# Part of a folded weight product placed inside attention's tiles

## The chip, the cores and the metric

The kernel runs on one core of a Trainium2 chip. The metric is device time in microseconds for one execution; three runs are given, and a profile of one further execution.

## The reference

Three layers follow one another, all in float32:

```python
# attention: 4 batches, 8 heads, 768 positions, 64 wide
state = gamma * state + outer(k[t], v[t]);  y[t] = scale * q[t] @ state
# mixture of experts: 3072 tokens of 512, 8 experts, 1024 wide inside
e = argmax(x @ w_gate + modality_bias[modality_id])
x = gate * (relu(x @ w1[e]) @ w2[e])
# last layer
out = ((x @ m_w1) * (x @ m_w2)) @ w3 @ w_out
```

Nothing stands between `w3` and `w_out`, so the kernel multiplies these two weights with each other ahead of time. This is the folded weight product.

## The kernel before

Attention works on 24 tiles of 128 positions, six to a batch. In a loop over tiles (lines 514 to 556) iteration t issues, in this order: the loads for tile t+6; `vprime` (values times a decay, GpSimd) for t+2; `scores(t+1)` on TensorE, masked by VectorE into `at`; `rows_gate(t-1)`, which turns the output `xT` into rows and gate logits; `attend_T` (queries times state) and `attend_v` (masked scores times values) of tile t, which go into one bank, from which VectorE scales them by a decay table into `xT` (line 333); and `state(t+1)`, whose sum ScalarE copies into `T`. Each engine takes its instructions in the order in which they were issued. A tile that begins a batch has no `attend_T`, and one that ends it has no `state`.

`rows_gate` has ScalarE copy the rows out and send them to HBM from its own queue. Its VectorE sum gives the gate logits `L`. After tiles 8, 15 and 21 of the count a batch of logits is routed: `route_a` and, an iteration later, `route_b` run as blocks of small VectorE operations, with two small products between. GpSimd then scatters each tile's tokens to their list positions in HBM (`scatter_ids`, line 398, 8 bytes a token).

The weights `w_out` and `w3` come as float64 bits in twelve chunks of 1 MB (0 to 3 and 4 to 11). VectorE decodes a chunk in three operations (lines 196, 198, 200). ScalarE casts it to a high part, and GpSimd or VectorE forms the low part. Seven chunks are decoded in attention's loop, five behind it. The folded product has 64 units of three 128x128x512 matmuls (line 245), eight units to a bank. All 64 run behind attention, in the fold stage:

```python
fold_mm(FM[0]); route_b(t0, t1)   # 6 units, then the last three tiles' routing
...                               # scatters, tables1 (list gather), one chunk decoded
tables2a(); fold_mm(FM[1]); tables2b()
...                               # first expert's weights, two chunks
fold_mm(FM[2]); tables3(); gather_x(0); gather_x(1)
...
t_x(0); fold_mm(64)               # the units that are left
```

`tables1` gathers the token lists from HBM by `ridx` (line 434), `tables2b` transposes the control table `c`, and `tables3` transposes the lists into gather indices. Then the first expert slot begins (line 234). Expert slots, the last layer's products and a tail follow.

PSUM has eight banks: five that `bank()` hands out in turn, one for the state and two for `rows_gate`.

## Time and profile before

| | us |
|---|---|
| median of three runs | 890.35 (890.24 to 890.61) |
| the profiled execution, its own time | 890.2 |
| its span, first to last instruction | 888.1 |
| TensorE matmul busy | 845.1 (95%) |
| VectorE busy | 479.6 (54%) |
| GpSimd busy | 341.7 (38%) |
| ScalarE busy | 287.8 (32%) |

Stretches are given in microseconds from the start of the span. Matmuls overlap in the pipeline, so the time from one start to the next says what one costs, not its length. PE is TensorE, DVE is VectorE, ACT is ScalarE, POOL is GpSimd, SP is SyncE, and a releaser is what ended an engine's idle time.

### The profile page before, as it was taken

The page shows a single profiled execution, that of the slowest core. Times are in us where ns is not written, and L with a number is a line of the kernel's source. Part 1 is how long each engine was busy: PE and PEld are TensorE (multiplying, and loading weights), DVE is VectorE, ACT ScalarE, POOL GpSimd, SP SyncE. Part 2 cuts the span into 40 slices and gives each one's busy share as a digit, 9 for nine tenths or more (in the row PEclk, how much of TensorE's full clock was granted, in tenths as well). Part 3 has the DMA queues.
Part 4 walks back from the last instruction along what each step waited for, and adds up shares of the span by engine and source line. Part 5 has one row for each costly group of instructions (what it writes and reads, how often), then busy time and mean ns, then how long its engine had stood idle before and what let it go on. Part 6 is the DMA issues. An engine that isn't in the chain of part 4 may idle for free. (4 is left out here: it accounts for less than half of the span.)

```text
span 888.1 us, 16214 instructions
## 1 busy us (share of the span) xinstructions
PE 845.1 (95%) x6240; PEld 771.9 (87%) x6240; DVE 479.6 (54%) x697; ACT 287.8 (32%) x514; POOL 341.7 (38%) x324
## 2 busy tenths in 40 slices
PE   5989798899999999999999979999999999999997
PEld 5978687679999999899999957887887888999996
DVE  4477675764432516751111662255236375999993
ACT  1232231143213233623111633232223353455541
POOL 4237374123005041804000314246326354656563
PEclk9998999999999999999999999999999999999999
DMA  8999974778236445744235039514111514644411
GB/s 297 348 389 232 337 183 109 202 265 314 88 121 214 144 169 191 275 179 180 84 96 216 26 123 410 218 48 147 63 51 60 148 51 146 225 168 154 143 49 59
DMA packets 63189, 153.68 MB, mean 173 GB/s; under 512 B 10676, under 2 KB 22964, under 8 KB 61545
## 3 DMA queue, kind: packets, MB, share of 16 engines
q1 hardware_dynamic: 51736, 122.64, 40.9%
q0 software_dynamic: 7888, 23.36, 7.5%
q10 hardware_dynamic: 3456, 6.29, 2.0%
q8 instruction: 61, 1.00, 0.5%
q14 instruction: 48, 0.39, 0.2%
HBM read 102.73 MB, written 49.58 MB: 171 GB/s over the span
## 5 line engine op out<-in xcount | busy, mean ns | idle before, releaser
L234 PE MATMUL b<-h,wh 128*128 128x256 f32 x768 | 139.7, 284 | 1.3 <-issue 0.7
L895 PE MATMUL al<-xh,ws 128*128 128x512 f32 x384 | 125.7, 397 | 5.3 <-PEq L868 3.6
L234 PEld LDWEIGHTS b<-h,wh 128*128 128x128 f32 x768 | 119.6, 192 | 1.7 <-issue 0.9
L759 DVE SCALAR_TENSOR_TENSOR h<-b,h 128x512 fp32r<-128x512 f32 x48 | 32.6, 689 | 157.7 <-ACT h L758 155.5
L234 PE MATMUL b<-xh,wl 128*128 128x256 f32 x384 | 108.7, 283 | 0.3 <-DVE wl L205 0.3
L234 PE MATMUL b<-xh,wh 128*128 128x256 f32 x384 | 108.8, 283 | 0.1
L234 PE MATMUL b<-h,wl 128*128 128x256 f32 x384 | 108.7, 283 | 0.1
L234 PE MATMUL b<-xl,wh 128*128 128x256 f32 x384 | 108.6, 283 | 0.0
L895 PEld LDWEIGHTS al<-xh,ws 128*128 128x128 f32 x384 | 73.0, 190 | 23.3 <-ACTq L868 3.8
L895 PE MATMUL al<-xl,ws 128*128 128x512 f32 x192 | 76.2, 397 | 0.0
L1095 PE MATMUL oa<-wfh,ab 128*128 128x256 f32 x384 | 75.0, 284 | 0.7 <-DVE ot L1102 0.6
L234 PEld LDWEIGHTS b<-xh,wl 128*128 128x128 f32 x384 | 73.6, 192 | 0.5 <-DVE wl L205 0.5
L234 PEld LDWEIGHTS b<-xh,wh 128*128 128x128 f32 x384 | 73.6, 192 | 0.4 <-issue 0.3
L234 PEld LDWEIGHTS b<-h,wl 128*128 128x128 f32 x384 | 73.6, 192 | 0.3 <-issue 0.3
L234 PEld LDWEIGHTS b<-xl,wh 128*128 128x128 f32 x384 | 73.6, 192 | 0.0
L1095 PEld LDWEIGHTS oa<-wfh,ab 128*128 128x128 f32 x384 | 61.6, 189 | 2.7 <-DVE ot L1102 2.2
L895 PE MATMUL ga<-xh,ws 128*128 128x512 f32 x192 | 63.4, 391 | 0.0
L758 ACT ACTIVATE h<-b 128x512 fp32r<-128x512 f32 x48 | 28.4, 597 | 86.4 <-PE b L234 84.9
L205 POOL TENSOR_TENSOR wo<-dec,wo 128x512 fp32r<-128x512 f32 x12 | 16.5, 1392 | 99.1 <-ACT wo L204 99.1
L1095 PE MATMUL oa<-wfl,ab 128*128 128x256 f32 x192 | 54.0, 281 | 0.0
L635 POOL DMA_INDIRECT xg<-x_scratch,gidx x28 | 28.4, 1014 | 64.6 <-PE b L644 44.4
L790 ACT COPY yT<-b 128x512 f32<-128x512 f32 x24 | 14.1, 589 | 118.3 <-PE b L234 110.7
(219 smaller groups left out, 1894.9 us busy)
## 6 DMA issues: line engine op xcount, KB each, us to landing
qkv<-in_qkv SPq DMA_DIRECT2D x22, 768.0 KB
ws_scratch<-wo SPq DMA_DIRECT2D x28, 512.0 KB
ws<-ws_scratch SPq DMA_DIRECT2D x28, 512.0 KB
raw<-in_wall SPq DMA_DIRECT2D x24, 512.0 KB
ab<-ab_scratch SPq DMA_DIRECT2D x24, 512.0 KB
f64f<-in_w SPq DMA_DIRECT2D x8, 1024.0 KB
f64m<-in_m SPq DMA_DIRECT2D x16, 512.0 KB
y_scratch<-yT SPq DMA_DIRECT2D x14, 512.0 KB
```

The source lines that it names most:

```text
L205: lo_eng.tensor_tensor(lo, src, hi.bitcast(F32), op=ALU.subtract)
L234: nc.tensor.matmul(b, lhsT=x, rhs=y, start=first and n == 0, stop=last and n == 3 * len(ks) - 1)
L635: nc.gpsimd.indirect_dma_start(out=xgs[j][y], out_offset=None, in_=xd, in_offset=bass.IndirectOffsetOnAxis(ap=gidx[:, y, j:j + 1], axis=0))
L758: nc.scalar.activation(h, b, AF.Relu)
L759: V.scalar_tensor_tensor(l, b, 0.0, h.bitcast(F32), op0=ALU.max, op1=ALU.subtract)
L790: nc.scalar.copy(yT[:, 2 * dp:2 * dp + 2, :].rearrange("p a t -> p (a t)"), b)
L895: nc.tensor.matmul(b, lhsT=y, rhs=r[:, kk, :], start=first and n == 0, stop=n == 5, skip_group_check=True)
L1095: nc.tensor.matmul(b, lhsT=x[:, k], rhs=y[:, k], start=first and n == 0, stop=n == 11, skip_group_check=True)
```

## The change

- Twelve chunks are loaded in attention's loop and ten are decoded there.
- From tile 15 on, each iteration issues three, three and two units of the folded product behind `scores`, 24 in all. They have a bank of their own, and four banks are handed out in turn.
- Decoding, the bias operations and routing become generators. `spend` issues their steps at the end of an iteration until the estimated costs reach `BUDGET[t]`.
- `decayed` scales the queries on VectorE ahead of `scores`, so `xT` (but for tile 0) is a plain copy by ScalarE.
- Row stores are issued by SyncE, with five buffers for three. Six loads of queries, keys and values are held instead of seven.
- Constants are loaded in pieces at the start, and the biases are formed from tile 3 on.
- The fold stage has 40 units and two chunks left, and `tables2a` follows `tables1` at once.

```diff
-LOAD_T = [2, 5, 8, 10, 13, 15, 18, 20, 22]
-SPLIT_T = [5, 8, 10, 13, 15, 18, 20]
-QB, KB, FB = 7, 5, 5
+LOAD_T = [1, 2, 5, 6, 8, 11, 12, 14, 16, 19, 21, 23]
+SPLIT_T = [3, 5, 7, 9, 11, 13, 15, 17, 19, 21]
+FOLD_T = 15
+FOLD_N = [3, 3, 2] * 3
+BUDGET = [2.0] * 14 + [2.6] * 11
+QB, KB, FB = 6, 5, 5
...
-FM = [6, 12, 8, 8, 8, 6]
+FM = [6, 8, 8, 6, 4, 4]
...
-        pss = [(ps, f"b{i}") for i in range(5)]
+        pss = [(ps, f"b{i}") for i in range(4)]
...
             V.scalar_tensor_tensor(d, s[:, :, 0], 29, d, op0=ALU.logical_shift_right, op1=ALU.bitwise_or)
+            yield
             yield from done(d.bitcast(F32))
...
-                b = bank()
+                b = ps.tile([P, 512], F32, tag="b4", name=f"fb{ic}") if len(pss) == 4 else bank()
...
+        def decayed(t, eng=V):
+            q = st[t]["qT"]
+            eng.tensor_tensor(q, q, gtab[t % NC], op=ALU.mult)
...
             s["xT"] = pa.tile([P, 4, P], F32, tag="xT", name=f"xT{t}", bufs=2)
-            V.tensor_tensor(s["xT"], b, gtab[t % NC], op=ALU.mult)
+            if t:
+                nc.scalar.copy(s["xT"], b)
+            else:
+                V.tensor_tensor(s["xT"], b, gtab[0], op=ALU.mult)
...
-            xr = pa.tile([P, 4, P], F32, tag="xr", name=f"xr{t}", bufs=3)
+            xr = pa.tile([P, 4, P], F32, tag="xr", name=f"xr{t}", bufs=5)
...
-            nc.scalar.dma_start(xd[t * P:t * P + P, :], xr.rearrange("p a w -> p (a w)"))
+            nc.sync.dma_start(xd[t * P:t * P + P, :], xr.rearrange("p a w -> p (a w)"))
...
         def route_a(t0, t1):
             sl, sh = slice(t0, t1), [P, t1 - t0, E]
             V.tensor_tensor(L[:, sl], L[:, sl], biasm[:, sl], op=ALU.add)
+            yield
             V.tensor_reduce(mx[:, sl, 0], L[:, sl], axis=AX.X, op=ALU.max)
...
             for t in range(t0, t1):
                 V.tensor_tensor(RS[:, t + 1, :], RS[:, t, :], OH[:, t, :], op=ALU.add)
+                yield
             V.tensor_tensor(tmp[1][:, sl], L[:, sl], bc(mx[:, sl], sh), op=ALU.subtract)
-            nc.scalar.activation(tmp[1][:, sl], tmp[1][:, sl], AF.Exp)
...
+            yield
+
+        def route_exp(t0, t1):
+            nc.scalar.activation(tmp[1][:, t0:t1], tmp[1][:, t0:t1], AF.Exp)
+
+        def route_mm(t0, t1):
+            sl, w = slice(t0, t1), (t1 - t0) * E
             b = bank()
             nc.tensor.matmul(b[:, :w], lhsT=CV("sl"), rhs=OH[:, sl].rearrange("p t e -> p (t e)"), start=True, stop=False)
             nc.tensor.matmul(b[:, :w], lhsT=CV("ones"), rhs=RS[:, sl].rearrange("p t e -> p (t e)"), start=False, stop=True)
+            return b
...
+        def route_b(t0, t1, b):
+            sl, sh, w = slice(t0, t1), [P, t1 - t0, E], (t1 - t0) * E
+            V.tensor_tensor(tmp[0][:, sl], b[:, :w].rearrange("p (t e) -> p t e", e=E), bc(CV("er").unsqueeze(1), sh), op=ALU.add)
+            yield
             V.tensor_reduce(dst[:, sl, 0], tmp[1][:, sl], axis=AX.X, op=ALU.add)
+            yield
...
             V.tensor_copy(dsti[:, sl], dst[:, sl, 0])
+            yield
...
+        cut, cid = CA["g"][0], CB["ident"][1]
         next(l0)
+        nc.sync.dma_start(ca[:, :cut], a["ca"][:, :cut])
+        run(l0)
+        nc.sync.dma_start(ca[:, cut:], a["ca"][:, cut:])
         next(l1)
-        nc.sync.dma_start(ca, a["ca"])
-        run(l0)
+        nc.sync.dma_start(cb[:, :cid], a["cb"][:, :cid])
+        nc.sync.dma_start(iwg[:, :, P:], a["wg"].rearrange("p (a e) -> p a e", a=4))
         run(l1)
...
+        def decays(c, eng=nc.gpsimd):
+            eng.tensor_tensor(gtab[c], gtab[0], bc(bd[:, c - 1].unsqueeze(2), [P, 4, P]), op=ALU.mult)
+
+        def prepare(t):
+            vprime(t)
+            if 2 < t < NC:
+                decays(t)
+
...
+        def late_loads():
+            nc.sync.dma_start(cb[:, cid:], a["cb"][:, cid:])
+            nc.sync.dma_start(mb.rearrange("p a e -> p (a e)"), a["mbias"].partition_broadcast(P))
+            nc.sync.dma_start(mod, a["mod"].bitcast(I32).rearrange("p (t two) -> p t two", two=2))
+            nc.sync.dma_start(tbl, nf)
+
+        def biases():
+            sh = [P, NTILE, E]
+            V.tensor_copy(mf[:, :, 0], mod[:, :, 0])
+            yield .8
+            V.tensor_tensor(biasm, bc(mf, sh), bc(mb[:, 1:2, :], sh), op=ALU.mult)
+            yield 1.1
...
+            V.tensor_copy(tg[:, :, 0], CV("tok"))
+            yield .2
...
+        def timed(g, costs):
+            for c in costs:
+                if next(g, g) is g:
+                    return
+                yield c
...
-        pend, work = [], iter(())
+        pend, ready, late, bg = [], [], [], deque()
+        small = itertools.repeat(.24)
+
+        def routed(t0, t1):
+            yield from timed(route_a(t0, t1), small)
+            ready.append((t0, t1))
+            yield 9.
+
+        def settled(t0, t1, b):
+            yield from timed(route_b(t0, t1, b), small)
+            pend.extend(range(t0, t1))
+
+        def decoded(g):
+            yield from timed(g, (.7, 1.2, 1.2))
+            late.append(g)
+
+        def finish():
+            for g in late:
+                run(g)
+            late.clear()
+
+        def spend(us):
+            while bg and us > 0:
+                c = next(bg[0], None)
+                if c is None:
+                    bg.popleft()
+                else:
+                    us -= c
+
+        def settle():
+            for r in ready:
+                route_exp(*r)
+                bg.appendleft(settled(*r, route_mm(*r)))
+            ready.clear()
+
         for t in range(-1, NTILE + 1):
-            for x in range(3, QB) if t == 0 else (t + QB - 1,):
-                if 0 < x < NTILE and t >= 0:
+            for x in {-1: (), 0: (3,), 1: (4, 5), 2: (6, 7)}.get(t, (t + QB - 1,)):
+                if x < NTILE:
                     run(load(x))
-            if 2 < t + 2 < NTILE:
-                vprime(t + 2)
+            if t == 2:
+                late_loads()
+            if 1 < t + 2 < NTILE and t >= 0:
+                prepare(t + 2)
+            finish()
             if t == -1:
                 scores(0)
-            if 1 <= t + 1 + (t < 0) < NTILE and t:
-                scores(t + 1 + (t < 0))
-            if t in SPLIT_T:
-                work = fold_split(SPLIT_T.index(t))
-            next(work, None)
-            if t - 1 >= 0:
+                decays(1, V)
+                decayed(1, V)
+                warm(4)
+            if 1 <= t and t + 1 < NTILE:
+                scores(t + 1)
+            if 0 <= t - FOLD_T < len(FOLD_N):
+                fold_mm(FOLD_N[t - FOLD_T], False)
+            if t >= 2:
                 rows_gate(t - 1)
+            settle()
             if 0 <= t < NTILE:
                 attend_T(t)
                 attend_v(t)
+            if t == 0:
+                scores(1)
+                V.tensor_copy(iwg[:, :, :P], bc(ident.unsqueeze(1), [P, 4, P]))
+                rows_gate(0)
             if t + 1 < NTILE:
                 state(t + 1)
-            next(work, None)
-            if t == -1:
-                V.tensor_copy(mf[:, :, 0], mod[:, :, 0])
-                sh = [P, NTILE, E]
-                V.tensor_tensor(biasm, bc(mf, sh), bc(mb[:, 1:2, :], sh), op=ALU.mult)
-                V.tensor_scalar(mf, mf, -1.0, 1.0, op0=ALU.mult, op1=ALU.add)
-                V.tensor_tensor(tmp[0], bc(mf, sh), bc(mb[:, 0:1, :], sh), op=ALU.mult)
-                V.tensor_tensor(biasm, biasm, tmp[0], op=ALU.add)
-                V.tensor_copy(tg[:, :, 0], CV("tok"))
-                V.tensor_copy(iwg[:, :, :P], bc(ident.unsqueeze(1), [P, 4, P]))
-            if t - 1 in bounds[1:-1]:
-                g = bounds.index(t - 1)
-                route_b(bounds[g - 1], bounds[g])
-                pend += list(range(bounds[g - 1], bounds[g]))
-            for _ in range(2):
+            fold_out()
+            for x in () if t < 0 else (t + 2,) if t < 4 else (6, 7) if t == 4 else (t + 3,):
+                if x < NTILE:
+                    decayed(x)
+            if t == 3:
+                bg.append(biases())
+            if t in SPLIT_T:
+                x = SPLIT_T.index(t)
+                bg.append(decoded(fold_split(x)))
+            if t in bounds[1:-1]:
+                g = bounds.index(t)
+                (bg.append if g < 3 else bg.appendleft)(routed(bounds[g - 1], bounds[g]))
+            if t >= 1:
+                spend(BUDGET[t])
+            for _ in range(2 if t < 23 else 3):
                 if pend:
                     scatter_ids(pend.pop(0))
-            if t in bounds[1:-1]:
-                g = bounds.index(t)
-                route_a(bounds[g - 1], bounds[g])
             if t in LOAD_T:
                 fold_load(LOAD_T.index(t))
-            next(work, None)
+        settle()
+        spend(99.)
+        finish()
         while pend:
             scatter_ids(pend.pop(0))
...
         t0, t1 = bounds[-2], bounds[-1]
-        route_a(t0, t1)
+        run(route_a(t0, t1))
+        route_exp(t0, t1)
         fold_mm(FM[0])
-        route_b(t0, t1)
+        run(route_b(t0, t1, route_mm(t0, t1)))
         for t in range(t0, t1):
...
-        pss += [(ps2, f"b{i}") for i in range(5, 7)]
+        pss += [(ps, "b4")] + [(ps2, f"b{i}") for i in range(5, 7)]
...
-        fold_a()
-        fold_b()
         tables2a()
         fold_mm(FM[1])
         tables2b()
@@ -660,25 +770,21 @@
         raw_load(expert(e0), range(4))
         fold_a()
         fold_b()
-        fold_a()
         fold_mm(FM[2])
         tables3()
         gather_x(0)
         gather_x(1)
         nc.gpsimd.memset(raw[4][:, :1], 0.0)
-        fold_b()
         fold_a()
         fold_b()
         fold_mm(FM[3])
         split_w(3)
         split_w(0)
         raw_load(expert(e0), range(4, 8))
-        fold_a()
-        fold_b()
         fold_mm(FM[4])
         split_w(1)
+        split_w(2)
         fold_mm(FM[5])
-        split_w(2)
         t_x(0)
         fold_mm(64)
         fold_mm(0)
```

The steps of `route_a` and `route_b` that are left out are as before, with a `yield` behind each.

## Rows read from the trace of the kernel before

**Rows 1.** Windows: stretch, then length, busy us (instructions) by engine, clock, DMA.
```profile
20.40:148.40 128.00, 113.75 (x1357) 104.14 (x1358) 84.03 (x174) 36.04 (x92) 60.69 (x68) 0.92 0.90 281
...
200.00:220.00 20.00, 20.00 (x168) 19.95 (x167) 10.05 (x17) 8.22 (x12) 8.09 (x6) 1.00 0.79 303
```

**Rows 2.** Timeline of TensorE, one steady tile: start, length, line, operation, matmuls merged.
```profile
27.02 1.19 PE L358 MATMUL r<-iwg,xT 128*128 128x136 f32 x8
28.05 1.05 PE L323 MATMUL b<-qkv,T 128*128 128x128 f32 x8
29.04 1.09 PE L331 MATMUL b<-at,vp 128*64 128x128 f32 x16
29.96 0.64 PE L347 MATMUL acc<-vp,qkv 128*64 128x64 f32 x16
30.53 1.16 PE L312 MATMUL b<-qkv,kT 64*128 64x128 f32 x16
31.62 1.19 PE L358 MATMUL r<-iwg,xT 128*128 128x136 f32 x8
```

**Rows 3.** Timeline of TensorE: three of the 24 row-and-gate products.
```profile
20.37 2.18 PE L358 MATMUL r<-iwg,xT 128*128 128x136 f32 x8 [4.60 <-DVE xT L333]
...
66.66 2.15 PE L358 MATMUL r<-iwg,xT 128*128 128x136 f32 x8 [0.91 <-DVE dst L384]
...
147.18 1.17 PE L358 MATMUL r<-iwg,xT 128*128 128x136 f32 x8 [1.35 <-DVE xT L333]
```

**Rows 4.** Timeline of TensorE and VectorE: tile 0's output product, biases, output scaling.
```profile
11.24 1.05 PE L331 MATMUL b<-at,vp 128*64 128x128 f32 x16
...
14.92 0.69 DVE L536 CAST mf<-mod_sb 128x24 f32<-128x24 int32 x1 [3.98 <-DMA mod_sb<-in_mod]
...
19.63 0.68 DVE L333 TENSOR_TENSOR xT<-b,ca_sb 128x512 f32<-128x512 f32 x1
```

**Rows 5.** Timeline of TensorE in the fold stage, to the first expert matmul.
```profile
148.41 0.40 PE L245 MATMUL b<-wol,w3h 128*128 128x512 f32 x1
...
152.04 0.40 PE L245 MATMUL b<-woh,w3l 128*128 128x512 f32 x1
...
165.12 0.69 PE L456 MATMUL b<-cb_sb,c 128*1 128x32 f32 x10 [3.82 <-DVE c L451]
...
200.18 0.28 PE L234 MATMUL b<-xh,wh 128*128 128x256 f32 x1
```

**Rows 6.** Timeline of VectorE and GpSimd around the index scatters and the list gather.
```profile
156.58 0.15 DVE L433 TENSOR_SCALAR ridx<-col_r 128x1 int32<-128x1 f32 x1
...
162.13 0.16 DVE L437 TENSOR_TENSOR rt_b<-rt_oh,rt_n 128x8 f32<-128x8 f32 x1
...
142.80 1.00 POOL L398 DMA_INDIRECT tok_scratch<-tg,dsti  x1 [7.22 <-DVE dsti L390]
...
156.46 1.01 POOL L398 DMA_INDIRECT tok_scratch<-tg,dsti  x1 [0.21 <-issue]
...
164.56 0.99 POOL L434 DMA_INDIRECT lists<-tok_scratch,ridx  x1 [7.09 <-DVE rt_a L448]
```

**Rows 7.** Windows: the DMA engines (last two columns) before and behind the scatters.
```profile
30.00:75.00 45.00, 41.95 (x525) 38.47 (x519) 31.01 (x64) 12.66 (x33) 17.74 (x18) 0.92 0.97 371
...
75.00:93.00 18.00, 16.88 (x236) 15.12 (x234) 13.27 (x20) 6.78 (x16) 12.61 (x15) 1.00 1.03 181
...
157.50:164.50 7.00, 3.80 (x17) 2.81 (x15) 5.51 (x16) 1.05 (x1) 0.00 (x0) 1.00 0.52 28
```

**Rows 8.** Groups by line and shape (mean ns), and one wait of VectorE.
```profile
L196 DVE TENSOR_SCALAR decf<-f64f 128x1024 uint32<-128x1024 uint32 x7 | 7.6, 1088 | 4.9 <-DMA f64f<-in_w 4.8
...
L198 DVE SCALAR_TENSOR_TENSOR decf<-f64f,decf 128x1024 uint32<-128x1024 uint32 x7 | 9.9, 1418 | 0.0
...
L261 ACT COPY wfo<-b 128x512 f32<-128x512 f32 x7 | 3.9, 593 | 0.0
...
100.79 0.69 DVE L196 TENSOR_SCALAR decf<-f64f 128x1024 uint32<-128x1024 uint32 x1 [4.85 <-DMA f64f<-in_w]
```

More of the change, by code (lines that the diff above doesn't have):

```diff
@@ L1 @@
 import itertools
+from collections import deque
 from contextlib import ExitStack
@@ L489 @@
         l0, l1 = load(0), load(1)
+        cut, cid = CA["g"][0], CB["ident"][1]
         next(l0)
+        nc.sync.dma_start(ca[:, :cut], a["ca"][:, :cut])
+        run(l0)
+        nc.sync.dma_start(ca[:, cut:], a["ca"][:, cut:])
         next(l1)
-        nc.sync.dma_start(ca, a["ca"])
-        run(l0)
+        nc.sync.dma_start(cb[:, :cid], a["cb"][:, :cid])
+        nc.sync.dma_start(iwg[:, :, P:], a["wg"].rearrange("p (a e) -> p a e", a=4))
         run(l1)
         bw = bank()
-        for _ in range(WARM):
-            nc.tensor.matmul(bw[:, :P], lhsT=wz, rhs=wz, start=True, stop=True)
@@ L498, with warm @@
-        nc.sync.dma_start(cb, a["cb"])
-        nc.sync.dma_start(iwg[:, :, P:], a["wg"].rearrange("p (a e) -> p a e", a=4))
+        def warm(n):
+            for _ in range(n):
+                nc.tensor.matmul(bw[:, :P], lhsT=wz, rhs=wz, start=True, stop=True)
+        def decays(c, eng=nc.gpsimd):
[4 more added lines that the diff above has]
+                decays(t)
@@ L500 @@
+        warm(WARM)
         run(load(2))
-        nc.sync.dma_start(mb.rearrange("p a e -> p (a e)"), a["mbias"].partition_broadcast(P))
-        nc.sync.dma_start(mod, a["mod"].bitcast(I32).rearrange("p (t two) -> p t two", two=2))
         vprime(0)
-        for c in range(1, NC):
-            nc.gpsimd.tensor_tensor(gtab[c], gtab[0], bc(bd[:, c - 1].unsqueeze(2), [P, 4, P]), op=ALU.mult)
-            if c < 3:
-                vprime(c)
+        decays(2)
+        vprime(1)
+        nf = none.rearrange("p i two -> p (i two)")
@@ L508 @@
         nc.sync.dma_start(xd[NT:NT + 1, :], Ts[1][0:1].rearrange("p a i -> p (a i)"))
-        nf = none.rearrange("p i two -> p (i two)")
-        nc.sync.dma_start(tbl, nf)
-        bounds = list(np.cumsum([0] + BATCHES))
-        pend, work = [], iter(())
+        def late_loads():
[3 more added lines that the diff above has]
+            nc.sync.dma_start(tbl, nf)
@@ new lines, in biases @@
+        def biases():
[4 more added lines that the diff above has]
+            yield 1.1
+            V.tensor_scalar(mf, mf, -1.0, 1.0, op0=ALU.mult, op1=ALU.add)
+            yield .8
+            V.tensor_tensor(tmp[0], bc(mf, sh), bc(mb[:, 0:1, :], sh), op=ALU.mult)
+            yield 1.1
+            V.tensor_tensor(biasm, biasm, tmp[0], op=ALU.add)
+            yield .4
+            V.tensor_copy(tg[:, :, 0], CV("tok"))
+            yield .2
```

13 lines of the change are left out of this document (9 added, 4 removed).

## The prediction

> **What bounds the kernel now.** Read the windows first [rows 1]: from 200 us on TensorE is busy in all of every stretch shown, so a microsecond saved ahead of the expert stage is a microsecond off the end, and nothing saved on another engine is. Ahead of it lie attention (to 148.35, the end of the last tile's row-and-gate product) and the fold stage (148.35 to 200.18, the first expert matmul).
>
> The timeline of one steady tile [rows 2] gives TensorE's own need: 4.60 us from one row-and-gate product to the next, of which state is 0.57, scores 1.09, the query-state product 0.99. Tile 0's product starts at 20.37 and tile 23's ends at 148.35 [rows 3]: 127.98 us. The need is 23 x 4.60 less three query-state products, five states and two scores that those tiles lack (8.0), plus the last product's 1.17: 99.0. So 29.0 us of attention are not TensorE's work. The row at 66.66 says what most are: TensorE waited on `dst`, a routing step of VectorE, and the same eight matmuls then took 2.15 us instead of 1.19, at the slow clock. VectorE runs its queue in order, and routing and decoding stand in front of the masks and the scaled outputs. The start is the same story [rows 4]: attention's product for tile 0 was through at 12.29, but its scaling ran at 19.63, behind six bias operations that began at 14.92, when their transfer had come.
>
> In the fold stage [rows 5] sixteen steps of the folded product take 3.63 us, 0.227 each, so a unit of three is 0.681 and 64 units are 43.6. The other 8.2 us of the 51.83 are a wait of 3.82 for the table `c`, and 4.4 of small products and slow clock.
>
> **The change, part by part.** *Units moved:* 24 x 0.681 = 16.35 us leave the fold stage and enter tiles 15 to 23, 1.8 us a tile. They fill idle time only if a tile has some; I add them to attention in full and ask separately what becomes of its 29.0.
>
> *Start:* biases go to tiles 3 and 4, and constants are loaded in pieces. From 12.29, 0.68 us of scaling [rows 4] and half a microsecond for the identity copy and the hand-over (an estimate) put tile 0's row product at 13.5, 6.9 us sooner. Bounds: nothing (the transfers still rule) and 8 (the product's own end).
>
> *Routing in small steps, placed at a tile's end under a budget:* the waits like 66.66 should go. Among the starts of the 24 row products (the first, the one at 66.66 and the last stand in [rows 3]) six intervals around the three routings carry 17.9 of the 29.0 us, each less its own need: 3.2, 2.8, 3.7, 1.6, 3.7, 2.9. I keep 3: the small products themselves and the tail of the last tile.
>
> *Decoding:* three more chunks run here, ten in all. In attention the first step costs 1.09 and the second 1.42 [rows 8], where the budget charges 0.7 and 1.2: 3.7 us a chunk for the 3.1 charged. Adding up the budget by hand, tiles 3 to 13 get six decodings, the biases and one routing, 28.2 us as charged and 31.8 at these prices. With 2.15 of masks, gate sum and query scaling a tile, VectorE needs (11 x 2.15 + 31.8)/11 = 5.0 us a tile, against 4.5 to 4.6 of TensorE. VectorE becomes the bound there by about 0.5 a tile: 5 us. From tile 15 on TensorE needs 6.4 and VectorE 4.8, so it is covered again. Bounds: 0 (masks are a tile ahead, which absorbs some) and 8.
>
> *Queries scaled ahead on VectorE, outputs copied by ScalarE:* 0.68 a tile comes and 0.68 goes on VectorE, nothing net; the scaling is two or three tiles ahead, and without that cover it would cost 0.68 x 23 = 16 us. The copy lies between attention's product and the row product. ScalarE copies 128x512 from PSUM in 0.593 [rows 8]; TensorE has state and scores to do meanwhile, 1.66 us, and ScalarE is busy 36 of 128 us [rows 1]. I charge nothing. The Trainium skill, "ScalarE: Activation LUTs", Rules for kernel authors, speaks against it: simple elementwise work belongs on VectorE, up to about three times as fast. By it the copy would take up to 2.1 us, 0.4 beyond its cover, 10 us over 23 tiles; the row (0.593 against VectorE's 0.68) doesn't bear this out.
>
> *Row stores to SyncE, five buffers; four rotating banks and one for the fold:* ScalarE loses 24 issues. On SyncE the store waits for its copy, and queued behind it are the loads for five tiles on and the next chunk; v-primes and decodings wait for those. With five tiles of lead that wait, under one tile, is covered; without the lead it would cost up to a tile, 4.6. A bank comes round after four takes, more than a tile, when its reader is done: nothing.
>
> *Transfers:* twelve chunks instead of nine are loaded here, and earlier. The DMA engines were 97% busy at 371 GB/s from 30 to 75 us, then gave 181 for 18 us, while eight index scatters went out [rows 7]. A decoding waits for its chunk, and in VectorE's queue masks and gate sums wait behind it; before, one such wait was 4.85 us [rows 8]. Sizes: the chunk for tile 13 stands behind 17 tiles, 5 other chunks, 11 row stores and constants, 28.1 MB. From 2.8 us at 371 GB/s with the 18 us dip inside, that has landed near 88; VectorE asks for it near 82. Masks are a tile ahead, which hides some 4 us, so I let 2 of the 6 reach TensorE, with bounds of 0 and 12. Gaps that no wait explains and slow clock, the other 11.1 us of the present 29.0 (2.0 of them at the start), I leave at 4.
>
> Attention then ends at 13.5 + 99.0 + 16.35 + 3 + 5 + 2 + 4 = 142.85, 5.5 earlier than now.
>
> *Fold stage:* 40 units are 27.2, the small rest 4.4. Table `c` no longer stands behind a decoding (156.66 to 162.13 on VectorE, 5.5 us [rows 6]), but TensorE comes 4 units sooner and the positions 0.5 later: the wait is 3.82 - 5.5 + 2.7 + 0.5 = 1.5. What is late next is the list gather. Nine scatters ran from 142.80, and the gather behind them started at 164.56 [rows 6], 21.76 later, 2.4 a scatter. The last of them was issued by 157.47 and ridx was ready at 156.73. In the gap the DMA engines moved 28 GB/s [rows 7], though a 1 MB load was issued there. So I read scatters as draining at 2.4 us. (The row names rt_a as releaser; were that right, the gather would follow the last scatter.) Now their first is later: in the last tile but one, some 1.5 ahead of attention's end instead of 5.5. The gather then starts 20.3 after that end and its list is there at 23.8 (1.0 to issue, 2.5 to land, an estimate between 0 and the 7.1 that the gather itself waited). TensorE has 22 units and small products done at 18.2: a wait of 5.6. Sum 27.2 + 4.4 + 1.5 + 5.6 = 38.7 instead of 51.83, 13.1 less. Bounds: 33 (no list wait) and 43.
>
> **Sum.** -5.5 - 13.1 = -18.6. The profiled execution took 890.2 with a span of 888.1, so 871.6, and since its time is 0.15 under the median of the runs, I say 871.5.
>
> **Rivals.**
> 1. *No wait in the tiles, list in time.* Masks a tile ahead absorb VectorE's surplus, and transfers keep up: 7 instead of 14 us above need, attention ends at 135.9 (-12.5). The gather follows its last scatter and the stage is 34 (-17.8). 860. For it: 371 GB/s holds the need until the scatters. Against it: [rows 7], the dip.
> 2. *Transfers pace tiles 3 to 16.* The chunk waits get through whole and several times (12 instead of 2, slow clock on top): attention ends near 152, 881. For it: 97% busy already with fewer chunks. Against it: from tile 17 on little is left to load.
> 3. *The ScalarE copy is slow.* 10 us more, 881. Against it: the 0.593.
> 4. *Slower.* The place is a decoding's wait for its chunk in VectorE's queue. Without such waits attention ends at 140.85; to lose the stage's 13.1 it must end at 161.4, which is 20.6 us, 2.1 through to TensorE for each of ten chunks. If each costs the 4.85 of [rows 8] less the 2 that a mask's lead hides, 28 us: attention ends at 169, 898. For it: one in seven did wait so long before. Against it: only the chunks near the scatters meet the dip.
>
> **How the numbers follow.** My forecast 0.55, rival 1 0.18, rival 2 0.14, rival 3 0.02, slower 0.07, and 0.04 for a loss in between that eats the gain to within 0.2% (1.8 us), about what a measurement of this kernel can tell from no change. Faster 0.89, same 0.04, slower 0.07. With its bounds my forecast alone spans 863 to 879; the range reaches past rival 1, whose stage may be another 1 shorter and its start 1 earlier, and past rival 2 by its slow clock: 857 to 884.
>
> **What would show it.** In the new trace: tile 0's row product near 13.5; the row products of tiles 3 to 13 about 5.0 us apart with VectorE nearly full; no wait on `dst`; 24 units between scores and row products from tile 15 on, 6.4 a tile; attention's end near 143; a TensorE wait of 5 to 6 us ahead of the list transposes; first expert matmul near 181.6. Wrong it would be by chunk waits on VectorE in most tiles, by a late attention end, or by lists that land at once.

## The result: slower by 0.9%, and the profile after

The changed kernel took 897.63 us (median of six runs, 896.23 to 900.34), the kernel before, beside it on the same chip, 890.3 (885.42 to 892.29). The ratio is 1.0087 with a 95% interval of 1.0064 to 1.0110. The forecast was 871.5 us.

TensorE's timeline of the changed kernel, to be read against [rows 2, 3, 5]: the row-and-gate products of tiles 0, 13 and 23, a state and a scores behind the first of them, three stalls before scores, two waits of the fold stage, and the first expert matmul.

```profile
13.85 1.96 PE L370 MATMUL r<-iwg,xT 128*128 128x136 f32 x7 [1.68 <-DVE iwg L643]
...
15.96 1.12 PE L359 MATMUL acc<-vp,qkv 128*64 128x64 f32 x16
18.10 1.16 PE L321 MATMUL b<-qkv,kT 64*128 64x128 f32 x16 [1.02 <-DVE qkv L312]
...
38.37 2.08 PE L321 MATMUL b<-qkv,kT 64*128 64x128 f32 x16 [3.21 <-issue]
...
59.43 1.16 PE L321 MATMUL b<-qkv,kT 64*128 64x128 f32 x14 [2.83 <-DVE at L323]
...
97.31 1.44 PE L321 MATMUL b<-qkv,kT 64*128 64x128 f32 x10 [5.06 <-DVE at L323]
...
99.31 1.95 PE L370 MATMUL r<-iwg,xT 128*128 128x136 f32 x7
...
163.07 1.19 PE L370 MATMUL r<-iwg,xT 128*128 128x136 f32 x8 [0.74 <-ACT xT L343]
...
184.30 0.61 PE L250 MATMUL b<-woh,w3h 128*128 128x512 f32 x1 [3.54 <-ACT wfo L266]
...
192.89 0.48 PE L495 MATMUL b<-cb_sb,lists 128*128 128x128 f32 x2 [2.62 <-DMA lists<-tok_scratch,ridx]
...
206.43 0.28 PE L239 MATMUL b<-xh,wh 128*128 128x256 f32 x1
```

Tile 0's row product came as forecast (13.85 for 13.5). Attention ended at 164.26 instead of 142.85, the fold stage took 42.2 instead of 38.7, and from the first expert matmul to the end it is 690.0 against 687.9 before. Of the 26.9 us between this span and the forecast one (869.5), 21.4 thus lie in attention, 3.5 in the stage, 2.1 behind it.

Where in attention? By the needs of [rows 2], tiles 0 to 13 cost TensorE 56.7 us of its own before (13 x 4.60 less two query-state products and two states). After it is 58.4, since the state and the scores at 15.96 and 18.10 now follow tile 0's product and stood ahead of it before. Tiles 13 to 23 cost 41.1 (10 x 4.60 less one query-state product, three states and two scores), and 57.4 with the 24 units. Before, the two stretches took 68.0 and 58.8 (tile 13's product began at 88.3); after, 85.5 and 63.8. So tiles 0 to 13 went from 11.3 us above need to 27.1, and tiles 13 to 23 from 17.7 to 6.3. The loss is early, before the first unit runs.

### The profile page after: what moved, and what is told of

Read it like the earlier page. It is cut to its first block, busy times and chain, and to the rows that moved or that the text cites. A ratio compares the mean times of both kernels' runs of the same rounds, so it can differ in the third digit from the quotient of the medians.

```text
span 896.4 us, 16307 instructions
## 1 busy us (share of the span) xinstructions
PE 847.8 (95%) x6248; PEld 773.6 (86%) x6248; DVE 488.4 (54%) x695; ACT 299.5 (33%) x537; POOL 352.1 (39%) x326
## 5 line engine op out<-in xcount | busy, mean ns | idle before, releaser
L864 ACT ACTIVATE h<-b 128x512 fp32r<-128x512 f32 x48 | 28.2, 597 | 84.0 <-PE b L239 82.5
```

What stands on the lines that cost most here:

```text
L864: nc.scalar.activation(h, b, AF.Relu)
```

## What stood in the early tiles

Groups by line and shape of the changed kernel (busy us, mean ns, idle time before them): query scaling, ScalarE's copy, first and second decoding step.

```profile
L312 DVE TENSOR_TENSOR qkv<-qkv,g 128x512 f32<-128x512 f32 x19 | 23.8, 1252 | 3.5 <-DMA qkv<-in_qkv 3.5
...
L343 ACT COPY xT<-b 128x512 f32<-128x512 f32 x23 | 13.5, 587 | 32.5 <-PE b L340 30.6 <-PE acc L359 2.0
...
L200 DVE TENSOR_SCALAR decf<-f64f 128x1024 uint32<-128x1024 uint32 x10 | 6.9, 688 | 10.3 <-POOL pad L430 10.3
...
L202 DVE SCALAR_TENSOR_TENSOR decf<-f64f,decf 128x1024 uint32<-128x1024 uint32 x10 | 14.8, 1485 | 0.3
```

ScalarE's copy is as priced (0.587). The scaling is not 0.68 but 1.25 on the mean. The timeline of VectorE and GpSimd at the first bias operation, ahead of and behind one such scaling, and at the longest wait of a decoding:

```profile
34.87 0.18 DVE L562 CAST mf<-mod_sb 128x24 f32<-128x24 int32 x1 [4.71 <-DMA mod_sb<-in_mod]
...
56.82 1.95 DVE L204 SCALAR_TENSOR_TENSOR decf<-f64f,decf 128x1024 uint32<-128x1024 uint32 x1
58.70 1.27 DVE L323 TENSOR_TENSOR at<-b,ca_sb 128x512 f32<-128x512 f32 x2
...
59.99 2.83 DVE L312 TENSOR_TENSOR qkv<-qkv,g 128x512 f32<-128x512 f32 x1
62.75 0.68 DVE L200 TENSOR_SCALAR decf<-f64f 128x1024 uint32<-128x1024 uint32 x1
...
93.44 0.69 DVE L200 TENSOR_SCALAR decf<-f64f 128x1024 uint32<-128x1024 uint32 x1 [5.56 <-POOL pad L430]
...
55.86 1.83 POOL L308 TENSOR_TENSOR vp<-qkv,ca_sb 128x512 f32<-128x512 f32 x1 [1.49 <-PE b L340]
59.93 2.35 POOL L225 TENSOR_TENSOR wol<-decf,woh 128x1024 fp32r<-128x1024 f32 x1 [2.24 <-ACT woh L223]
...
91.06 2.35 POOL L225 TENSOR_TENSOR wol<-decf,woh 128x1024 fp32r<-128x1024 f32 x1
93.34 0.09 POOL L430 MEMSET pad<- 1x1 f32 x1
```

Three things are to be seen. GpSimd begins the low part of a chunk at 59.93; the scaling, which reads queries and decay table from SBUF, begins 0.06 later and ends at 62.82, 0.54 behind GpSimd's end. That is a wait for the other engine's whole instruction, not a slower pace, and it recurs at 52.08, 67.89 and 97.87. Both instructions follow the end of a decoding, the low part behind a cast of 1.04 us, the scaling behind two masks of 1.27 together. The scaling that it replaced read PSUM and took 0.67 to 0.69 in all 24 tiles, also beside subtractions (0.68 at 48.87, with GpSimd on a low part from 48.14 to 50.50). The Trainium skill, "SBUF — State Buffer", Who interferes with whom, states just this: a VectorE instruction with two SBUF inputs contends with a GpSimd instruction that reads SBUF, and whichever comes second waits for the whole of the first. The trace agrees (2.83 for 0.68 beside 2.35); the prediction had not used it.

And at 93.44 a decoding has waited 5.56 us. The row names the memset at 93.34, but its chunk had long been there: there is one `dec` buffer, and the low part of the chunk before it ended at 93.41. GpSimd had it in its queue behind two scatters and a product of values. Masks for TensorE's scores at 97.31 stood behind that wait.

The third is the first in time. At 34.87 VectorE had waited 4.71 us for the modality ids, which the biases of tile 3 need. Masks and the scaling of tile 6's queries (37.59 to 38.26) stood behind them, and TensorE began the next scores at 38.37, after 3.21 us of idle time for which its row names no releaser. From there to 44.20 its granted clock was 0.50, the lower level.

## Theories and runs

Theory 1: VectorE standing behind GpSimd makes masks late. Theory 2: loads and SyncE's queue pace tiles 3 to 14. Theory 3: units cost their full price in the tiles, and the stage gives back only part. Theory 4: the single decode buffer. Theory 5: the bytes, with the scatters' gap in them.

In the table, "stretch" is the sum, over VectorE's instructions from 12 to 168 us, of each one's time less the shortest of its line and shape (two expectations below name 18.7 for e_dec2 and 12.0 for e_dps, from a coarser count). Times are starts of first weight loads in the profiled execution. Tile 14's has the first three units in it, 2.0 us at full clock, but not in the kernel before, e_no_units, e_seven, e_shift and e_shift1. The ratio (95% interval) is to the kernel before, beside it on the same chip.

| run | ratio | tile 13 | tile 14 | tile 23 | first expert | stretch |
|---|---|---|---|---|---|---|
| before | 1 | 88.3 | 95.1 | 147.2 | 200.0 | 5.4 |
| after | 1.0087 (1.0064 to 1.0110) | 99.3 | 107.5 | 163.1 | 206.2 | 18.6 |
| e_psum_scale | 1.0103 (1.0079 to 1.0127) | 99.4 | 107.9 | 163.3 | 206.1 | 4.1 |
| e_load_late | 1.0082 (1.0055 to 1.0108) | 98.0 | 106.9 | 161.8 | 202.2 | 10.9 |
| e_psum_late | 1.0087 (1.0064 to 1.0111) | 99.8 | 108.1 | 163.6 | 205.4 | 4.3 |
| e_no_units | 1.0143 (1.0120 to 1.0167) | 98.8 | 105.0 | 154.2 | 208.6 | 16.5 |
| e_dec2 | 1.0084 (1.0051 to 1.0117) | 91.8 | 102.4 | 157.8 | 198.1 | 17.9 |
| e_dec2_psum | 1.0004 (0.9979 to 1.0028) | 86.9 | 102.4 | 156.7 | 198.7 | 8.2 |
| e_dec2_psum_bias | 1.0068 (1.0047 to 1.0090) | 83.5 | 103.5 | 159.5 | 203.2 | 9.6 |
| e_seven | 1.0125 (1.0072 to 1.0178) | 85.2 | 95.8 | 139.7 | 200.9 | 13.0 |
| e_scat | 1.0088 (1.0062 to 1.0114) | 100.3 | 109.2 | 164.1 | 204.7 | 19.6 |
| e_qb7 | 1.0089 (1.0062 to 1.0117) | 97.6 | 106.4 | 161.4 | 203.4 | 12.3 |
| e_dps | 0.9986 (0.9963 to 1.0010) | 87.7 | 96.1 | 150.8 | 192.9 | 11.6 |
| e_shift | 1.0049 (1.0026 to 1.0071) | 84.5 | 91.1 | 148.4 | 202.8 | 8.6 |
| e_ps | 1.0061 (1.0039 to 1.0083) | 96.5 | 104.7 | 160.2 | 202.8 | 5.0 |
| e_ds | 1.0035 (1.0018 to 1.0053) | 91.7 | 100.8 | 155.0 | 196.4 | 25.3 |
| e_dps_bias | 1.0053 (1.0033 to 1.0074) | 84.9 | 98.1 | 160.5 | 202.8 | 19.6 |
| e_shift1 | 1.0019 (1.0008 to 1.0031) | 84.9 | 91.7 | 153.4 | 197.8 | 11.6 |
| e_dec2_love | 1.0061 (1.0037 to 1.0084) | 89.8 | 103.9 | 159.3 | 200.7 | 10.1 |
| e_dps_love | 0.9965 (0.9943 to 0.9987) | 85.4 | 94.2 | 148.6 | 191.8 | 4.1 |

One profile is one execution, and a kernel's executions spread by about 1% (e_dec2: 890.5 to 901.2; its profile and e_seven's are their fastest executions, e_dec2_psum's its slowest): verdicts go by the ratios, causes by the rows.

### One cause at a time

```diff
-            if t:
-                nc.scalar.copy(s["xT"], b)
-            else:
-                V.tensor_tensor(s["xT"], b, gtab[0], op=ALU.mult)
+            V.tensor_tensor(s["xT"], b, gtab[t % NC], op=ALU.mult)
...
-                decayed(1, V)
...
-                    decayed(x)
```

> The changed kernel with the query scaling put back: VectorE scales the product tile out of PSUM, as before the change, and neither the scaling of the queries in SBUF nor ScalarE's copy is there. Theory 1 (in tiles 5 to 8 and 12 VectorE's scaling of two SBUF operands, 0.68 us by itself, stands behind GpSimd's subtraction of a decoded chunk, 2.35 us, and takes 2.84, so that masks come 2.2 late): the scaling takes 0.69 also beside a subtraction, the stalls before scores that end with a mask (1.5, 2.8 and 2.8 us at 50, 57 and 64 us) shrink below 1 each, and with the clock that they cost the time falls by 6 to 12, to 886 to 892. Theory 2 (the chunk loads and the transfers behind them pace tiles 3 to 14, the scaling only fills a wait): the stalls stay in sum, 895 to 899.

Measured: 1.0103, no gain, though the stretch fell from 18.6 to 4.1. VectorE, GpSimd and TensorE of this run:

```profile
52.63 1.52 DVE L200 TENSOR_SCALAR decf<-f64f 128x1024 uint32<-128x1024 uint32 x1 [7.18 <-POOL wol L225]
...
57.88 0.68 DVE L342 TENSOR_TENSOR xT<-b,g 128x512 f32<-128x512 f32 x1
...
46.07 1.04 POOL L308 TENSOR_TENSOR vp<-qkv,ca_sb 128x512 f32<-128x512 f32 x1 [11.26 <-DMA qkv<-in_qkv]
...
49.26 1.04 POOL L308 TENSOR_TENSOR vp<-qkv,ca_sb 128x512 f32<-128x512 f32 x1 [2.14 <-PE b L332]
50.26 2.34 POOL L225 TENSOR_TENSOR wol<-decf,woh 128x1024 fp32r<-128x1024 f32 x1
...
57.82 2.35 POOL L225 TENSOR_TENSOR wol<-decf,woh 128x1024 fp32r<-128x1024 f32 x1 [4.22 <-ACT woh L223]
...
57.32 2.07 PE L321 MATMUL b<-qkv,kT 64*128 64x128 f32 x14 [6.23 <-DVE at L323]
```

At 57.88 the scaling out of PSUM takes 0.68 beside a low part that began at 57.82: the mechanism of theory 1 is shown. But tiles 4 to 6, which begin 3 to 5.5 us sooner, run into the next wait: a decoding stood 7.18 us for the buffer, since the low part stood behind products of values that waited for loads and TensorE. Waits ahead of the ten decodings rose from 10.3 to 20.0 us. As the cause of the time theory 1 alone falls.

```diff
-LOAD_T = [1, 2, 5, 6, 8, 11, 12, 14, 16, 19, 21, 23]
+LOAD_T = [1, 2, 5, 7, 9, 11, 13, 15, 17, 19, 21, 23]
```

> The changed kernel with six chunk loads issued one tile later, each after the decoding that frees its buffer, so that SyncE's queue does not stand on it with the loads of queries and rows behind. Theory 2 (SyncE's waits for decodings, 28 us in sum, make the loads behind them late): the stall of 5.1 us at 92 us and the slow clock behind it go, the time falls by 5 to 9, to 888 to 893. Theory 1: the three stalls behind masks in tiles 5 to 8 stay as they are, and the time is within 2 us of the changed kernel.

Measured: 1.0082, no gain, tile 13 only 1.3 sooner; SyncE's waits for decodings fell from 28.2 to 17.7 us.

Both edits together:

> The changed kernel with both edits: scaling out of PSUM and the six chunk loads one tile later. Theory 1 alone: as with the scaling alone, 886 to 892. Theory 2 alone: as with the loads alone, 888 to 893. Both, each with stalls of its own: 878 to 886, and no stall over 2 us before the scores of tiles 4 to 14 but the one at 35 us that waits for the modality ids.

Measured: 1.0087, none of the cases. Theory 2 in this form falls.

```diff
-            return f64_f32(fold, "dec", f64t.pop(x), f"f{x}", done, 1)
+            return f64_f32(pa if x % 2 and x < 10 else fold, "dec", f64t.pop(x), f"f{x}", done, 1)
...
-            xr = pa.tile([P, 4, P], F32, tag="xr", name=f"xr{t}", bufs=5)
+            xr = pa.tile([P, 4, P], F32, tag="xr", name=f"xr{t}", bufs=4)
```

> The changed kernel with a second buffer for a decoded chunk (odd chunks in a buffer of their own that lives through attention; rows' copies have four buffers instead of five to make room). Theory 4 (a decoding cannot begin before GpSimd's subtraction of the chunk before it, since there is one buffer; VectorE stands in its queue meanwhile, with the masks behind): VectorE's waits of 5.6 us at 93 and 4.8 at 142 before the first step of a decoding go, the stall of 5.1 us of TensorE at 92 with them, and the time falls by 4 to 9, to a ratio to the kernel before of 0.999 to 1.004. Theory 1 (VectorE's scaling behind GpSimd's subtraction): the three stalls at 50, 57 and 64 us stay. Theory 2 (transfers): nothing over 2 us is gained, the row product of tile 13 begins at 98 to 100 again.

Measured: the waits before decodings are gone (0.0 of 10.3) and tile 13 begins 7.5 sooner, but tile 14 only 5.1, and the ratio, 1.0084, shows no gain. The wait is real and not alone.

### Units, and the spacing of the decodings

```diff
-FOLD_N = [3, 3, 2] * 3
+FOLD_N = []               # 64 units behind attention, nine chunks decoded
...
```

> The changed kernel with no unit of the weight product in the tiles (all 64 after attention, in shares of 6, 10, 8, 8, 8, 8 and the rest) and nine chunks decoded in attention instead of ten. Theory 3 (from tile 15 on TensorE has no idle time, so that each unit costs its 0.68 us there, and after attention the chain of scatters, lists and decodings sets the pace, so that a unit taken away there gives back only part): attention ends about 16 us sooner, near 148, the stage after it is 10 to 16 longer, and the whole is 1 to 6 us faster than the changed kernel, 891 to 897. Rival (the units stand in waits, as the change means them to): attention ends less than 8 sooner, the stage is 16 longer, and the whole is 905 to 912.

Measured: 1.0143, slower than the changed kernel; neither case, but the rival's direction. Tiles 13 to 23 took 55.5 us against 63.8 in the changed kernel: 24 units, and a tenth decoding, cost 8.3 where the units alone need 16.35, so half of them stood in idle time. The stage took 53.3 instead of 42.2. Windows of the stage of the changed kernel, then of this run (length, busy us by engine):

```profile
164.30:206.20 41.90, 33.42 (x146) 26.17 (x145) 26.67 (x65) 10.82 (x16) 18.33 (x23) 0.92 0.55 157
```

```profile
155.40:208.55 53.15, 47.95 (x219) 39.22 (x217) 28.05 (x69) 12.29 (x19) 16.40 (x22) 0.94 0.46 164
```

With 24 units elsewhere TensorE is busy 14.5 us less in the stage. Moving units and one decoding was worth some 0.5%; theory 3 falls.

With no units and the kernel before's schedule (nine loads, seven decodings):

> The changed kernel with no unit in the tiles and the kernel before's schedule of loads and decodings: nine loads and seven decodings, spaced by two or three tiles, the other five chunks and all 64 units after attention. It keeps the shortened start, the scaling of the queries, ScalarE's copy and the row stores on SyncE's queue. If the ten closely spaced decodings are what costs in tiles 3 to 13: the row product of tile 13 begins at 80 to 86, attention ends near 140 and the whole is 881 to 886, a ratio of 0.993 to 0.998. If it is the scaling, the copy or the stores: tile 13 at 93 or later and a ratio over 1.0.

Measured: tile 13 at 85.2 and tile 23's product at 139.7, as the first case says, so scaling, copy and stores don't hold tiles 3 to 13 without the close decodings. But the ratio is 1.0125: the stage took 60.2 us and the first expert came at 200.9. TensorE waited there 5.7 for the table `c` and 5.1 for a copy-out, the expectation having taken the stage as it was.

### Together

e_dec2 and e_psum_scale in one:

> The second buffer for a decoded chunk and the scaling out of PSUM together. Theories 1 and 4 each with a stall of its own, the one hidden while the other stands (the scaling alone moved the stall to a decoding that waited 7.2 us for GpSimd): all stalls of TensorE before the scores in tiles 4 to 13 are under 2 us but the one at 35, the row product of tile 13 begins at 85 to 91 instead of 99.3, and the time falls by 9 to 16, to a ratio of 0.991 to 0.999. Theory 2: the row product of tile 13 begins at 97 or later.

Measured: 1.0004, so 0.8% comes back where each alone gave nothing. Tile 13 begins at 86.9, as theories 1 and 4 say; then 15.5 us pass to tile 14, with a stall of 6.05 before scores at 96.97. VectorE of this run there, and GpSimd:

```profile
89.78 0.69 DVE L200 TENSOR_SCALAR decf<-f64f 128x1024 uint32<-128x1024 uint32 x1 [2.96 <-DMA f64f<-in_w]
90.51 4.55 DVE L202 SCALAR_TENSOR_TENSOR decf<-f64f,decf 128x1024 uint32<-128x1024 uint32 x1
...
90.63 1.05 POOL L308 TENSOR_TENSOR vp<-qkv,ca_sb 128x512 f32<-128x512 f32 x1
...
91.63 2.34 POOL L225 TENSOR_TENSOR w3l<-decf,w3h 128x1024 fp32r<-128x1024 f32 x1
```

A chunk is late by 2.96, and the next step, two SBUF operands again, ends only behind two GpSimd instructions in a row.

With six chunk loads later, and the biases queued from tile 6:

> As the run with the second buffer and the scaling out of PSUM, with the six chunk loads a tile later and the six bias instructions queued three tiles later, so that VectorE does not wait for the modality ids. If the wait for the ids (4.7 us of VectorE at 35) still ends on TensorE: the stall of 3.2 us at 35 goes and the time is 3 to 6 below the run without these two; if transfers have become the pace there, less than 2.

Measured: 1.0068, slower. The stall at 35 went (tile 4 1.5 sooner), but a later chunk left the first units waiting 11.0 us at 100 for a low part.

```diff
-            for _ in range(2 if t < 23 else 3):
+            for _ in range(0 if t < 14 else 2 if t < 23 else 3):   # scatters
```

> The changed kernel with no scatter of token ids before tile 14: the first eight, which begin at 79 us two to a tile, wait until then. Theory 5 (the transfers pace tiles 4 to 14: every variant so far has tile 14's row product at 102 to 107 whatever its engines do, and while the first eight scatters run, 80 to 90 us, only 116 GB/s are moved, with the loads of the tiles ahead standing in the same queues): over 300 GB/s are moved from 80 to 90, the row product of tile 14 begins 5 to 9 sooner than 107.5, and the time falls by 4 to 9. Rival, theory 4 (VectorE's waits for the one decoded-chunk buffer): GpSimd's subtraction no longer stands behind scatters, so the wait of 5.6 us at 93 goes too, and the two are told apart by the rows: with 4 alone, tile 14's row product begins 3 to 5 sooner and the moved bytes from 80 to 90 don't matter.

Measured: 1.0088, no gain; from 80 to 90 us 181 GB/s moved instead of 116, not 300.

> The second buffer for a decoded chunk, the scaling out of PSUM, and no scatter before tile 14. Theory 5: where the run without the last edit had tile 14's row product at 102.4, after a wait of 10 us behind tile 13, it begins at 92 to 96, and the time falls by 4 to 9 against that run, to a ratio to the kernel before of 0.990 to 0.996. If the waits behind decodings alone set the pace: less than 2 is gained.

Measured: 0.9986, less gain than said; tile 14 begins at 96.1, some 6 sooner than in e_dec2_psum, at the edge of what was said. The ratios' intervals overlap, so what the scatters' move is worth by itself is not settled. Windows of this run:

```profile
35.00:70.00 35.00, 28.11 (x344) 25.94 (x344) 27.05 (x53) 10.84 (x26) 12.95 (x8) 0.90 1.00 386
70.00:80.00 10.00, 10.00 (x148) 9.20 (x150) 8.48 (x19) 2.64 (x8) 3.09 (x3) 1.00 0.59 217
80.00:90.00 10.00, 7.83 (x85) 7.13 (x82) 9.90 (x10) 4.14 (x9) 8.51 (x6) 0.92 0.92 335
```

From 35 to 70 the DMA engines are fully busy at 386 GB/s. A tile's loads and rows (1.31 MB) and half a chunk (0.52) are 1.83 MB, 4.7 us at that rate by this estimate: what TensorE needs. Nothing would be left over to catch up a wait.

Seven buffers for loads, three for rows, on the changed kernel:

> The changed kernel with seven buffers of queries, keys and values as in the kernel before, instead of six (rows' copies have three instead of five to make room). If the shorter lead of the loads is what leaves tiles 4 to 14 waiting: tile 14's row product begins 4 to 8 sooner than 107.5 and the time falls as much. Theory 5 (the bytes themselves, not the lead): less than 2.

Measured: 1.0089; tile 14 1.1 sooner. The shorter lead is not the cause by itself.

e_dps with loads and decodings two tiles later, units from tile 17, nine decodings:

> As the run with the second buffer, the scaling out of PSUM and no early scatter, with the decodings moved two tiles later (from tile 5 on, nine of them) and the chunk loads and the 24 units with them (units from tile 17 on); three chunks are left for the stage after attention instead of two. About two chunks, 2.1 MB, fewer are moved before tile 13. Theory 5: tile 14's row product begins another 3 to 6 sooner, 87 to 92; attention ends at 150 to 154, the stage after it is 2 longer for the third chunk, and the time is another 1 to 4 below, a ratio of 0.986 to 0.994. If decodings and masks on VectorE set the pace: no gain over the run without the move.

Measured: tile 14 at 91.1, 5 sooner; but 2.0 of that are the three units that no longer stand ahead of it. Tile 13, which had no unit in either, is 3.2 sooner, the low end of what theory 5 says, and attention's end 2.4. But with a third chunk the stage took 53.5 against 41.1, not 2 more. TensorE waited 5.1 of that for casts of decoded chunks, which it did not wait for in e_dps. Ratio 1.0049. Three chunks made 53 us with 40 units as with 64 (e_no_units); the kernel before did five in 51.8. So the number of units alone doesn't set the stage's length; that the placing of the chunks does is argued, not shown.

The pairs that were left:

> The changed kernel with the scaling out of PSUM and no scatter before tile 14, and one buffer for a decoded chunk. If the single buffer holds the tiles by itself once the scaling is gone (a decoding waits for GpSimd's subtraction, which waits in its queue behind products of values that have not landed): a wait of 5 us or more before a decoding stays, and the ratio to the kernel before is over 1.005. If the scaling was the cause and the buffer only a stand-in: 0.997 to 1.003, as with all three.

Measured: 1.0061, with waits of 17.3 us before decodings. Against e_dps (0.9986) the buffer is needed.

> The changed kernel with the second buffer for a decoded chunk and no scatter before tile 14; VectorE scales the queries in SBUF as in the changed kernel. If the scaling behind the subtraction holds the tiles by itself once the buffer is there: three or more stalls of 1.4 to 3 us behind masks stay between 50 and 100 us, ratio over 1.004. If not: 0.997 to 1.003.

Measured: 1.0035, with a stretch of 25.3. Against e_dps (0.9986) the scaling in SBUF costs 0.5% once buffer and scatters are out of the way.

e_dps with the biases queued two tiles later:

> All three edits, and the six bias instructions queued two tiles later. If the wait for the modality ids (4.7 us of VectorE at 33 us) ends on TensorE: its stall of about 2.3 us there goes, and 2 to 4 us of the whole with it against the run with three edits. If the bytes are the pace by then: the row product of tile 14 moves by less than 1.5 us and the whole by less than 1.

Measured: 1.0053, slower; tile 4 begins 1.9 sooner, as said, and tile 14 2 later. VectorE, then GpSimd, near tile 16:

```profile
110.52 0.67 DVE L342 TENSOR_TENSOR xT<-b,g 128x512 f32<-128x512 f32 x1
111.11 3.80 DVE L377 TENSOR_TENSOR L<-L,biasm 128x56 f32<-128x56 f32 x1
...
111.47 1.05 POOL L308 TENSOR_TENSOR vp<-qkv,ca_sb 128x512 f32<-128x512 f32 x1
112.48 2.36 POOL L225 TENSOR_TENSOR w3l<-decf,w3h 128x1024 fp32r<-128x1024 f32 x1
```

An addition of 56 elements took 3.80; in the changed kernel one of 64 took 0.21 at 70.64. A saving of 2 us early moved which instruction meets GpSimd here; that this is the whole loss is not shown.

e_dps_bias with loads, decodings and units one tile later:

> All three edits, the bias instructions two tiles later, and loads and decodings one tile later, ten of them kept, with the 24 units in tiles 16 to 23. If the bytes are the pace from tile 4 to 14 (one chunk fewer by tile 13, 1 MB or 2.6 us at 405 GB/s): the row product of tile 14 begins at 91 to 94 and attention ends 1 to 4 sooner than in the run with three edits (151.8); the stage keeps its 41; the whole is 2 to 5 lower, a ratio of 0.993 to 0.997. If VectorE is the pace: no gain.

Measured: 1.0019; tile 14 at 91.7 as said, but without the units' 2.0, then 12 us to tile 15 with them, and attention's end 2.6 later than in e_dps. Against e_dps nothing is gained. Against e_dps_bias, from which this run differs by the shift alone, 0.3% is (the intervals don't overlap) and attention ends 7.1 sooner, so fewer early bytes did help there.

```diff
-                bg.append(decoded(fold_split(x)))
+                bg.append(decoded(fold_split(x, V)))
-            finish()
+            for g in late:      # the cast
+                next(g)
...
+            finish()            # the low part, ahead of spend()
```

On e_dec2, then on e_dps:

> The run with the second buffer for a decoded chunk (scaling in SBUF, scatters as in the changed kernel; ratio 1.0084) with the low parts of the ten chunks subtracted by VectorE at the end of a tile instead of by GpSimd. VectorE does 10 x 1.2 us more of its own. Theory 1 (VectorE stands behind GpSimd's subtraction wherever an instruction reads two SBUF operands): the scalings take 0.68 to 1.4 everywhere, what VectorE's instructions take over their shortest falls from 18.7 us to under 8, and the time falls by 3 to 7, ratio 1.000 to 1.005, though VectorE has 12 us more to do. Rival (its own work sets the pace, the stretching costs nothing): 1.008 or more.

> All three edits (ratio 0.9986) with the low parts subtracted by VectorE at the end of a tile. Theory 1: what VectorE's instructions take over their shortest falls from 12.0 us to under 5, no stall over 3 us before scores is left in tiles 4 to 14 but behind transfers, ratio 0.990 to 0.997, faster than the kernel before. If the bytes are the pace by then: 0.997 to 1.001, and VectorE waits for chunks instead.

Measured: 1.0061 (not 1.005 or less) and 0.9965, stretch 10.1 (not under 8) and 4.1. In the first, with no low part on GpSimd, the scaling of two SBUF operands takes 0.67 to 0.69 in all rows but two (1.31 and 1.52), as theory 1 says. The second beats both kernels: against the kernel before by 0.35% (0.13 to 0.57), though VectorE does ten more subtractions of 1.3 us. Its windows from tile 0's row product to tile 13's and on to attention's end:

```profile
13.14:85.40 72.26, 64.45 (x820) 58.97 (x821) 51.29 (x99) 22.14 (x56) 20.75 (x20) 0.95 0.92 349
85.40:149.80 64.40, 61.12 (x641) 54.11 (x642) 46.19 (x98) 18.15 (x44) 25.90 (x37) 1.00 0.92 243
```

Tiles 0 to 13 are 13.9 above need instead of 27.1. The intervals with and without this last edit overlap, so its own share is not settled.

## Why the prediction was wrong

- **The step that failed: VectorE's sum for tiles 3 to 13, in two terms that leave out waits for GpSimd.** The runs show these two waits in its place. Undoing either alone gives nothing (1.0103, 1.0084), both together 0.8%, with the scatters' move 1.0%.
- **First term: queries scaled ahead, "0.68 a tile comes and 0.68 goes on VectorE, nothing net".** It priced the instruction by time and not by where its operands lie. The new one is 10.9 us longer in sum, of 18.6 of stretch: 8.6 beside GpSimd's subtractions, 2.3 beside other work of GpSimd, mostly products of values. The first form read PSUM and took 0.67 to 0.69 in every row. The means that I took as durations of decoding steps (1088 and 1418 ns, [rows 8]) had such waits in them: their shortest are 0.67 and 1.21.
- **Second term: decoding, "VectorE becomes the bound there by about 0.5 a tile: 5 us", bounds 0 to 8.** Right engine and tiles, far too small: 27.1 - 11.3 = 15.8 us more above need, where routing waits were to go as well. Left out was that a decoding needs the buffer of the one before, and so waits for GpSimd's queue: 10.3 us in two waits. e_seven, with seven decodings and the scaling kept, has tile 13 at 85.2.
- **Start:** the biases in tiles 3 and 4 were charged by their length alone; the wait for the modality ids (4.71 on VectorE, 3.21 of idle time on TensorE behind it) was not seen. Queueing them later takes that stall away, but no time. And the 99.0 of need lacks the state and the scores, 1.66, that now come behind tile 0's product.
- **Rival 4** had the place (a decoding's wait in VectorE's queue, masks behind) and the sign, but named the chunk's transfer. Its 898 meets the measured 897.63 by luck: it has attention's end 4.7 us later than measured, and stage and rest 5.6 sooner. In the profile the long waits are for GpSimd; chunk waits show only where those are gone (2.96 in e_dec2_psum, 5.4 in e_dps). **Rival 2** has a part in that second layer, as e_dps's windows and e_shift1 say; how large, no run settles.
- **Units "in full", 16.35.** Too dear: 8.3 with a tenth decoding, for tiles 13 to 23 still had idle time.
- **Fold stage 38.7.** 42.2. The gather began 21.2 behind attention's end (forecast 20.3), at 2.57 a scatter, so lists held TensorE 2.6 and not 5.6; not seen were 3.5 for a copy-out behind a cast on ScalarE, and a wait of 2.3 for the counts `rt_n`.
- **Right:** tile 0's row product, ScalarE's copy (0.587), the routing waits on `dst`, which are gone. The figure of the Trainium skill, "ScalarE: Activation LUTs", Rules for kernel authors, that the prediction set against the copy is given there for bf16 with one source; this copy is fp32 out of PSUM, and 2.1 us does not follow from it.
- **A slip without weight:** the last step of the sum takes 0.15 off, where a profiled execution under the median asks for it to be added: 871.75.

What this explains is the loss, not the whole miss. With the three edits of e_dps the loss of 0.9% is gone, yet attention ends at 152.0 and the stage takes 41.1; even e_dps_love has its first expert matmul at 192.0, where 181.6 was forecast. Some 1.8% of the forecast 2.1% stay out of reach of all runs.

Open: where those lie; how the 0.9% divides, since the waits cover one another; what the row stores on SyncE and the fifth bank cost, since no run puts them back (SyncE waited 31.3 us in sum for row copies, where the prediction charged nothing); why the part behind the first expert matmul varies between 687 and 693 us from run to run; and how much of tiles 4 to 14 the bytes would hold by themselves.

## What to carry to other kernels

Price an instruction by what runs beside it as well as by its length: on VectorE, moving an operand from PSUM to SBUF made 0.69 us into 2.84 beside a subtraction of GpSimd. Before adding work to an engine that serves the bound in order, list every buffer and queue that the new work waits for; a wait that another wait covers can't be found by undoing one edit, so undo pairs. And ask where in time idle lies: the units went where some was left, the decodings where there was little.

## Not expected of the hardware

VectorE's first decoding step, one SBUF operand, 0.67 at best, was stretched as well: 1.52 at 52.63 in e_psum_scale, with GpSimd on a low part until 52.60 and a product of values from 52.55. The Trainium skill, "SBUF — State Buffer", Who interferes with whom, allows for it: such operations have a mode that uses the port shared with GpSimd. No view here tells which mode ran. The masks, which read one operand from PSUM, stayed at 0.67 to 0.69 a piece in every run.

The two longest stretches shown, 4.55 at 90.51 in e_dec2_psum and 3.80 at 111.11 in e_dps_bias, began by their rows 0.12 and 0.36 ahead of GpSimd's product, while a scatter ran on GpSimd, and yet ended behind the subtraction after it. So the order of the starts doesn't tell there who waits; why is open.
